# New engine orders for a fused attention and gated feed-forward kernel

## Chip, cores and metric

The kernel runs on one core of one Trainium2 chip. The metric is device time in microseconds (us), the median of several executions. The engines are named as in the profile: PE (TensorE, with PEld for its weight loads), DVE (VectorE), ACT (ScalarE), POOL (GpSimd), SP (SyncE, which here only issues DMAs).

## The reference

Two branches work on the same input x (2048 tokens of 512 numbers, bf16) and are mixed by a gate per token. Shortened:

```python
g = sigmoid((x * gate_w).sum(-1))              # one number per token
out = g * A(x) + (1 - g) * B(x)

def B(x):                                       # 512 -> 1792 -> 512
    return (gelu(x @ w_gate) * (x @ w_up)) @ w_down

def A(x):                                       # 32 heads of 16, 4 segments of 512 tokens
    q, k, v = x @ wq, x @ wk, x @ wv            # per head and segment
    for s in range(4):
        p = softmax(q_s @ k_s.T / 4 + causal mask)
        a_dot = p @ v_s
        a_mem = (phi(q_s) @ M) / (phi(q_s) @ z + 1e-6)     # memory of earlier segments
        o_s = sigmoid(beta) * a_mem + (1 - sigmoid(beta)) * a_dot
        M, z = M + phi(k_s).T @ v_s, z + phi(k_s).sum()
    return o @ wo                               # phi(t) = t + 1 if t > 0 else exp(t)
```

## The kernel before

The program works in four segments of 512 tokens and is one straight stream of instructions per engine, without loops on the chip. The build cuts the work into 630 named PE tasks and some 580 named tasks of the other engines. A written list per engine, `ORDER`, says in which order each engine works its tasks off. Each engine takes its list strictly in order; a task that must wait holds back all that stand behind it on its engine. The waits themselves are semaphores that `Emitter` places from the reads and writes of the tasks, so another order is another set of waits for the same work.

The names on PE, with segment first: `K0_2.1`, `Q1_3.0`, `V0_1.2` are pieces of the projections (piece .0 uses the first two blocks of 128 of the 512 input columns, piece .2 the last two; in segment 0 the K pieces are single matmuls of 256 columns). `G` and `U` are the gate and up projections (14 column tiles each), `D` the output of a token tile (its pieces take `wo` times attention, then `wd` times the feed-forward; in the last segment the other way round). `num` is phi(q) times the memory, `mz` the sum of phi(k) times v, 128 PE instructions in a row. `qk1_2A0` is a score fill: eight small matmuls (32 for a low fill, `L`) on four row groups of the array, into the four PSUM banks `psXALL`. `pv1_2_0` is a P*V task of 32 matmuls. Each matmul is two instructions on PE, the weight load and the matmul.

All tasks but the score fills share four more PSUM banks, `psW`. A bank is given to a task's group when its first piece comes up, and it is free again when a copy on ACT or DVE has read it: `Kev`, `Qev`, `Vev`, `Gev` are such copies, `Um` multiplies the up projection into the gelu, `pvt` transposes P*V, `fin` scales an output tile. Many copies may be on ACT or on DVE, and the two lists decide it.

Each fill is read by one exp (`exp1_2A0`, ACT) over all four banks of `psXALL`, so the next fill must wait for it; POOL then masks the result (`msk`). Between two fills PE usually has five pieces. Once per segment ACT changes to gelu and back, with a table load each way.

On SP stand the loads of x and of the weights (wk and wq are issued on ACT; `x2_1` loads one quarter of segment 2's x with a DMA transpose, `xt1` loads segment 1's x untransposed), copies within the chip (`pkT`, `oTd` transpose, `Vlo` copies V rows) and the stores (`out`). A load of w_up, w_down, wo or x2 has a "tick" among its reads: it waits for a named exp, so that loads don't all go out at once. `Vlow` and the x buffers are reused by later segments, and their loads wait for the last reader.

`Sched.schedule` walks the lists with estimated costs. With the lists given, its estimates decide only which of the four banks each group gets and in which order tasks of different engines are entered. Among its constants are `BLOCK`, `BLOCK_ASK` and `BLOCK_END` (when PE's code is fetched), `DMA_RATE`, and the byte counts that are passed with each load.

Of the kernel before, what the change touches and what calls it, by code (L numbers as in the profile page):

```python
# [7 lines left out]
PE, ACT, DVE, POOL, SP = "pe", "act", "dve", "pool", "sp"  # L8
# [26 lines left out]
BLOCK, BLOCK_ASK, BLOCK_END = 256, 165, 208  # L35
# [3 lines left out]
        "K0_2.0 K0_3.0 K0_0.1 K0_1.1 K0_2.1 K0_3.1 x0t0_1 x0t1_1 K0_0.2 K0_0.3 K0_2.2 K0_3.2 K0_2.3 K0_1.2 K0_1.3 "  # L39
        "K0_1.4 K0_1.5 K0_1.6 K0_1.7 K0_0.4 K0_0.5 K0_0.6 K0_0.7 K0_3.3 K0_2.4 K0_2.5 K0_2.6 K0_3.4 K0_3.5 Q0_2.0 "  # L40
        "Q0_1.0 Q0_1.2 Q0_2.2 Q0_3.0 K0_2.7 Q0_3.2 K0_3.6 Q0_0.0 Q0_0.2 K0_3.7 V0_1.0 V0_1.2 V0_0.0 V0_0.2 "
        "qk0_0A0 G0_5.0 G0_5.2 V0_3.0 V0_2.0 V0_2.2 qk0_0B0 V0_3.2 Q1_3.0 Q1_3.2 G1_10.0 G1_10.2 qk0_0L G0_1.0 "
        "G0_1.2 G0_9.0 G0_9.2 G0_7.0 qk0_0A1 G1_9.0 Q1_0.0 G0_4.0 G1_9.2 G0_4.2 qk0_0B1 G0_7.2 G1_7.0 G1_7.2 "
        "Q1_0.2 G1_1.0 G1_1.2 qk0_1A0 G1_11.0 G1_5.0 G1_5.2 G1_11.2 Q1_1.0 qk0_1B0 G0_6.0 G1_2.0 Q1_1.2 G0_10.0 "
        "G1_2.2 qk0_1A1 G0_6.2 K1_2.0 G0_10.2 pv0_0_1 pv0_0_0 qk0_1B1 K1_2.2 K1_1.0 G1_8.0 Q1_2.0 Q1_2.2 qk0_2A0 "
        "G1_8.2 K1_1.2 G0_8.0 G0_8.2 G0_3.0 qk0_2B0 V1_2.0 G0_3.2 V1_2.2 pv0_1_1 pv0_1_0 qk0_2L mz0 V1_0.0 "
        "G0_13.0 V1_0.2 qk0_2A1 G0_13.2 V1_3.0 G1_12.0 V1_3.2 G0_2.0 qk0_2B1 G1_12.2 G1_0.0 G0_2.2 G1_0.2 G0_0.0 "
        "G0_0.2 qk0_3A0 K1_0.0 G1_6.0 G1_6.2 K1_0.2 G0_12.0 qk0_3B0 K1_3.0 G0_12.2 K1_3.2 Q2_2.0 Q2_2.2 qk0_3A1 "
        "G1_3.0 G1_3.2 G0_11.0 G0_11.2 pv0_2_1 pv0_2_0 qk0_3B1 V1_1.0 Q2_0.0 Q2_0.2 Q2_3.0 Q2_3.2 G1_13.0 V1_1.2 "
        "G1_4.0 G1_4.2 G1_13.2 U0_1.0 U0_1.2 U0_2.0 U0_4.0 U0_2.2 U0_9.0 U0_0.0 U0_4.2 U0_0.2 qk1_0A0 U0_9.2 "  # L50
        "U0_3.0 U0_3.2 U0_7.0 U0_7.2 U0_10.0 U0_8.0 U0_8.2 U0_13.0 U0_13.2 U1_0.0 U1_0.2 U0_5.0 U0_10.2 U0_5.2 "
        "U1_13.0 num1_00.0 U1_1.0 U1_1.2 U1_10.0 U1_13.2 U1_10.2 U0_6.0 U1_7.0 U0_6.2 U1_5.0 U1_7.2 U1_2.0 "
        "qk1_0B0 U1_5.2 U1_2.2 U1_11.0 pv0_3_0 pv0_3_1 qk1_0L U0_11.0 Q2_1.0 Q2_1.2 U1_3.0 U0_11.2 qk1_0A1 U1_3.2 "
        "D0_0.0 D0_0.2 num1_01.0 D0_0.4 U1_11.2 qk1_0B1 U0_12.0 num1_02.0 U0_12.2 D0_0.6 D0_0.8 D0_2.0 qk1_1A0 "
        "D0_0.10 U1_8.0 U1_6.0 U1_8.2 U1_6.2 D0_0.12 qk1_1B0 D0_0.14 D0_2.2 D0_0.16 D0_2.4 D0_2.6 qk1_1A1 D0_2.8 "
        "num1_12.0 num1_10.0 num1_11.0 D0_2.10 D0_2.12 D0_2.14 qk1_1B1 D0_2.16 U1_12.0 U1_9.0 U1_9.2 U1_12.2 "
        "qk1_2A0 pv1_0_0 pv1_0_1 pv1_1_1 mz1 pv1_1_0 qk1_2B0 D0_1.0 D0_1.2 D0_1.4 D0_1.6 D0_1.8 V2_3.0 qk1_2L "
        "D0_1.10 D0_1.12 D0_1.14 D0_1.16 V2_3.2 qk1_2A1 V2_0.0 D0_3.0 U1_4.0 K2_0.0 U1_4.2 qk1_2B1 V2_0.2 D0_3.2 "
        "K2_3.0 D0_3.4 K2_0.2 qk1_3A0 K2_3.2 K2_1.0 D0_3.6 K2_2.0 K2_1.2 qk1_3B0 K2_2.2 D0_3.8 V2_1.0 D0_3.10 "
        "D0_3.12 qk1_3A1 D0_3.14 D0_3.16 V2_1.2 Q3_1.0 Q3_1.2 G2_0.0 qk1_3B1 pv1_2_0 pv1_2_1 G2_0.2 G2_1.0 G2_3.0 "  # L60
        "G2_2.0 G2_3.2 G2_1.2 G2_2.2 G2_6.0 G2_6.2 G2_7.0 G2_4.0 G2_4.2 G2_5.0 G2_5.2 qk2_0A0 pv1_3_0 pv1_3_1 "
        "G2_7.2 G2_8.0 G2_10.0 G2_8.2 G2_10.2 G2_9.0 G2_9.2 G2_11.0 G2_12.0 G2_11.2 G2_12.2 G2_13.0 G2_13.2 "
        "U2_9.0 U2_9.2 num2_01.0 U2_8.0 U2_8.2 D1_0.0 D1_0.2 num2_00.0 D1_0.4 U2_13.0 U2_13.2 qk2_0B0 num2_02.0 "
        "D1_0.6 D1_0.8 D1_0.10 D1_0.12 D1_0.14 U2_6.0 qk2_0L D1_0.16 U2_3.0 U2_0.0 U2_0.2 U2_6.2 qk2_0A1 U2_3.2 "
        "Q3_0.0 V2_2.0 D1_2.0 V2_2.2 qk2_0B1 Q3_0.2 num2_11.0 num2_10.0 D1_2.2 D1_2.4 D1_2.6 D1_2.8 qk2_1A0 "
        "Q3_3.0 Q3_3.2 D1_2.10 D1_2.12 U2_10.0 qk2_1B0 V3_0.0 U2_10.2 V3_0.2 Q3_2.0 Q3_2.2 qk2_1A1 U2_1.0 U2_7.0 "
        "num2_12.0 U2_7.2 D1_2.14 U2_1.2 qk2_1B1 V3_3.0 V3_3.2 U2_4.0 U2_4.2 D1_2.16 qk2_2A0 mz2 pv2_0_0 pv2_0_1 "
        "pv2_1_0 pv2_1_1 qk2_2B0 D1_3.0 D1_1.0 D1_1.2 D1_1.4 D1_1.6 qk2_2L D1_1.8 D1_3.2 D1_1.10 D1_3.4 V3_1.0 "
        "qk2_2A1 V3_1.2 D1_3.6 K3_2.0 D1_1.12 D1_3.8 qk2_2B1 D1_1.14 D1_3.10 K3_2.2 D1_1.16 K3_3.0 qk2_3A0 "
        "D1_3.12 U2_11.0 U2_11.2 K3_3.2 D1_3.14 qk2_3B0 K3_1.0 K3_1.2 V3_2.0 D1_3.16 K3_0.0 qk2_3A1 K3_0.2 G3_0.0 "  # L70
        "U2_5.0 U2_5.2 U2_12.0 V3_2.2 U2_12.2 qk2_3B1 pv2_2_1 pv2_2_0 G3_0.2 G3_1.0 G3_1.2 G3_2.0 G3_3.0 G3_3.2 "
        "G3_2.2 G3_4.0 G3_4.2 G3_8.0 G3_5.0 G3_5.2 G3_6.0 G3_6.2 G3_7.0 G3_9.0 G3_7.2 G3_9.2 G3_8.2 G3_10.0 "
        "G3_10.2 G3_12.0 G3_11.0 G3_11.2 G3_12.2 G3_13.0 G3_13.2 U3_5.0 qk3_0A0 U3_5.2 U3_9.0 U2_2.0 U3_7.0 "
        "U3_7.2 U2_2.2 U3_9.2 U3_10.0 qk3_0B0 pv2_3_1 pv2_3_0 U3_10.2 U3_4.0 qk3_0L U3_3.0 U3_3.2 U3_8.0 D2_0.0 "
        "U3_8.2 qk3_0A1 U3_4.2 D2_0.2 D2_0.4 D2_0.6 D2_0.8 qk3_0B1 num3_00.0 D2_0.10 num3_02.0 U3_2.0 U3_2.2 "
        "D2_0.12 num3_01.0 qk3_1A0 D2_0.14 D2_0.16 U3_6.0 D2_1.0 D2_1.2 qk3_1B0 D2_1.4 U3_6.2 D2_1.6 U3_0.0 "
        "U3_0.2 num3_10.0 qk3_1A1 U3_13.0 num3_11.0 U3_13.2 D2_1.8 D2_1.10 D2_1.12 num3_12.0 qk3_1B1 D2_3.0 "
        "D2_1.14 D2_3.2 D2_1.16 U3_1.0 qk3_2A0 pv3_0_0 pv3_0_1 D2_3.4 D2_3.6 U3_1.2 qk3_2B0 D2_3.8 D2_2.0 pv3_1_0 "
        "pv3_1_1 qk3_2L D2_3.10 D2_2.2 D2_3.12 D2_2.4 D2_3.14 qk3_2A1 D2_3.16 D3_0.0 D3_0.2 U3_12.0 D2_2.6 "
        "qk3_2B1 D2_2.8 U3_11.0 U3_11.2 D2_2.10 D2_2.12 qk3_3A0 D3_1.0 D3_0.4 D3_0.6 D2_2.14 D2_2.16 qk3_3B0 "  # L80
        "D3_1.2 U3_12.2 D3_0.8 D3_0.10 D3_1.4 qk3_3A1 pv3_2_0 pv3_2_1 D3_1.6 D3_2.0 qk3_3B1 pv3_3_0 D3_0.12 "
        "D3_2.2 D3_1.8 D3_2.4 D3_3w1.0 D3_1.10 D3_3w1.4 pv3_3_1 D3_3w1.8 D3_2.6 D3_0.14 D3_2.8 D3_1.12 D3_3w0.0 "
        "D3_3w1.12 D3_1.14 D3_3w0.4 D3_0.16 D3_1.16 D3_3w0.8 D3_2.10 D3_3a1.0 D3_2.12 D3_2.14 D3_2.16 D3_3w0.12 "
        "D3_3a0.0 "),
    "act": (
        "w_wk0 w_wk1 w_wq0 w_wq1 tload K0_0even K0_0ev pke0_0 Q0_2ev kl0_01 Q0_3ev kl0_21 kl0_20 Vev0_1 K0_3ev "
        "exp0_0A0 kl0_00 exp0_0B0 gexp Vev0_2 exp0_0L Gev0_1 exp0_0A1 gsum0_2 exp0_0B1 pke0_1 exp0_1A0 gexs0 "
        "exp0_1B0 Q1_1ev exp0_1A1 pqe1_0 exp0_1B1 K1_2ev exp0_2A0 Gev0_8 exp0_2B0 pqe1_1 exp0_2L Gev0_3 exp0_2A1 "
        "Vev1_3 exp0_2B1 Gev1_0 Gev0_2 exp0_3A0 K1_0ev exp0_3B0 Gev0_0 exp0_3A1 Q2_2ev gexs1 Gev0_11 exp0_3B1 "
        "gelu0_0 Gev1_4 gelu0_2 gelu0_6 gelu0_10 gelu1_0 gelu1_7 exp1_0A0 kl1_01 exp1_0B0 exp1_0L Q2_1ev exp1_0A1 "  # L90
        "pke1_0 exp1_0B1 exp1_1A0 pke1_1 exp1_1B0 fin0_0 exp1_1A1 exp1_1B1 fin0_2 exp1_2A0 pqe2_0 exp1_2B0 pqe2_1 "
        "exp1_2L fin0_1 exp1_2A1 exp1_2B1 gsum2_1 exp1_3A0 exp1_3B0 K2_3ev K2_2ev exp1_3A1 gexs2 exp1_3B1 gelu2_0 "
        "gelu2_1 gelu2_2 gelu2_3 gelu2_4 gelu2_5 gelu2_6 gelu2_7 kl2_00 gelu2_8 gelu2_9 gelu2_10 gelu2_11 "
        "gelu2_12 gelu2_13 exp2_0A0 exp2_0B0 pke2_0 exp2_0L fin1_0 exp2_0A1 pke2_1 exp2_0B1 Q3_0ev exp2_1A0 "
        "exp2_1B0 exp2_1A1 exp2_1B1 exp2_2A0 pqe3_0 exp2_2B0 exp2_2L exp2_2A1 Vev3_1 exp2_2B1 K3_2ev exp2_3A0 "
        "K3_3ev exp2_3B0 gsum3_2 exp2_3A1 pqe3_1 gexs3 exp2_3B1 gelu3_0 gelu3_1 gelu3_2 gelu3_3 gelu3_4 gelu3_5 "
        "gelu3_6 kl3_01 gelu3_7 gelu3_8 gelu3_9 gelu3_10 gelu3_11 gelu3_12 gelu3_13 exp3_0A0 exp3_0B0 exp3_0L "
        "exp3_0A1 exp3_0B1 exp3_1A0 fin2_0 exp3_1B0 exp3_1A1 exp3_1B1 fin2_1 exp3_2A0 exp3_2B0 exp3_2L exp3_2A1 "
        "exp3_2B1 exp3_3A0 exp3_3B0 fin2_2 exp3_3A1 exp3_3B1 fin3_0 fin3_30 "),
# [1076 lines left out]
```

## Time and profile before

| | |
|---|---|
| time, median of 3 | 270.37 us (269.36 to 270.85) |
| the profiled execution | 270.25 us |
| its span, first to last instruction | 268.5 us |
| granted TensorE clock | 1.0 |
| PE busy | 262.4 us (98%), 3021 matmuls |
| ACT busy | 210.5 us (78%) |
| DVE busy | 202.2 us (75%) |
| POOL busy | 105.1 us (39%) |
| DMA | 18.23 MB, mean 68 GB/s |
| read from HBM, written | 9.84 MB, 2.10 MB |

A line of the timeline gives the start and the length in us, the engine, the source line, the operation, what is written and read, the shape, the number of instructions merged, and in brackets the idle time ahead with what ended it. "issue" there means that the engine waited for nothing that the profile shows. Most matmuls come from one helper, so they share line 497; fills are line 860, exps 866, P*V 908 and 916, `mz` 828, copies 511 (ACT) and 514 (DVE). Ends of matmuls are modelled, so the distance from start to start is the better measure of PE.

### The profile page before, as it was taken

The page shows a single profiled execution, that of the slowest core. Times are in us where ns is not written, and L with a number is a line of the kernel's source. Part 1 is how long each engine was busy: PE and PEld are TensorE (multiplying, and loading weights), DVE is VectorE, ACT ScalarE, POOL GpSimd, SP SyncE. Part 2 cuts the span into 40 slices and gives each one's busy share as a digit, 9 for nine tenths or more (in the row PEclk, how much of TensorE's full clock was granted, in tenths as well). Part 3 has the DMA queues.
Part 4 walks back from the last instruction along what each step waited for, and adds up shares of the span by engine and source line. Part 5 has one row for each costly group of instructions (what it writes and reads, how often), then busy time and mean ns, then how long its engine had stood idle before and what let it go on. Part 6 is the DMA issues. An engine that isn't in the chain of part 4 may idle for free.

```text
span 268.5 us, 7155 instructions
## 1 busy us (share of the span) xinstructions
PE 262.4 (98%) x3021; PEld 119.2 (44%) x3021; DVE 202.2 (75%) x399; ACT 210.5 (78%) x180; POOL 105.1 (39%) x256
## 2 busy tenths in 40 slices
PE   8999999999999999899999999999999999999995
PEld 4543345334444435433444443543444444443452
DVE  1689989878988897868985877897691885685662
ACT  2689899989998987788868897779888768776801
POOL 8106582785200346161520628313771072326310
DMA  6950732892000055520000146230000002400002
GB/s 221 319 148 0 172 89 24 256 295 78 2 0 2 1 85 126 147 63 2 0 2 0 22 88 75 61 101 20 2 1 2 2 0 62 99 23 22 22 1 78
DMA packets 32752, 18.23 MB, mean 68 GB/s; under 512 B 20560, under 2 KB 32720, under 8 KB 32720
## 3 DMA queue, kind: packets, MB, share of 16 engines
q1 hardware_dynamic: 31632, 16.73, 25.6%
q10 hardware_dynamic: 1088, 1.05, 1.2%
q8 instruction: 23, 0.38, 0.6%
q14 instruction: 9, 0.07, 0.1%
HBM read 9.84 MB, written 2.10 MB: 44 GB/s over the span
## 4 chain that ended last, share of the span: by engine, by line
PE 90%; DMA 5%; SPq 2%; ACT 1%; issue 1%; ACTq 1%
PE psW L497 71%; PE psXALL L860 9%; PE psW L908 6%; DMA wq<-in_A_wq_dram 3%; PE psXALL L497 3%; DMA xT<-in_A_x_dram 2%; SPq L524 2%; PE psW L916 1%; ACT ptl L866 1%; ACTq L528 1%; PE psW L828 0%; SPq L528 0%; ACT ost L1036 0%; ACT hT L511 0%; ACTq L393 0%
## 5 line engine op out<-in xcount | busy, mean ns | idle before, releaser
L866 ACT ACTIVATE pt<-psXALL 128x2048 bf16<-128x2048 f32 x64 | 120.1, 1877 | 27.3 <-PE psXALL L860 24.5
L869 POOL TENSOR_SCALAR_AFFINE_SELECT pt<-pt 128x256 bf16<-128x256 bf16 x128 | 55.3, 443 | 111.9 <-ACT pt L866 107.0
L497 PE MATMUL psW<-xT,wu 128*128 128x512 bf16 x224 | 55.9, 380 | 0.0
L497 PE MATMUL psW<-wd,hT 128*128 128x512 bf16 x210 | 55.3, 380 | 0.0
L497 PE MATMUL psW<-xT,wg 128*128 128x512 bf16 x224 | 53.7, 380 | 0.0
L1007 DVE TENSOR_TENSOR hT<-psW,hT 128x512 bf16<-128x512 f32 x56 | 37.1, 684 | 19.1 <-PE psW L497 18.8
L869 POOL TENSOR_SCALAR_AFFINE_SELECT ptl<-ptl 128x512 bf16<-128x512 bf16 x32 | 23.9, 746 | 29.1 <-ACT ptl L866 27.4
L497 PEld LDWEIGHTS psW<-xT,wg 128*128 128x128 bf16 x224 | 20.6, 98 | 25.8 <-issue 1.9
L497 PEld LDWEIGHTS psW<-xT,wu 128*128 128x128 bf16 x224 | 20.7, 98 | 24.2 <-issue 1.7
L497 PEld LDWEIGHTS psW<-wd,hT 128*128 128x128 bf16 x210 | 18.4, 98 | 21.2 <-issue 2.7
L922 DVE STREAM_TRANSPOSE tb<-psW 128x512 f32<-128x512 f32 x32 | 21.7, 701 | 8.0 <-PE psW L916 7.7
L860 PE MATMUL psXALL<-qT,kpad 32*128 32x320 bf16 (+3 forms) x512 | 25.7, 273 | 1.3 <-issue 1.3
L860 PEld LDWEIGHTS psXALL<-qT,kpad 32*128 32x128 bf16 x512 | 7.7, 92 | 26.3 <-ACT pt L866 15.7
L908 PE MATMUL psW<-pt,vaug 128*17 128x192 bf16 (+3 forms) x512 | 18.8, 273 | 0.0
L991 ACT ACTIVATE hT<-psW 128x512 bf16<-128x512 f32 x28 | 15.3, 596 | 4.5 <-PE psW L497 4.5
L771 POOL COPY exsT<-exs 32x4 f32<-32x4 f32 x64 | 15.4, 240 | 8.2 <-ACT exs L762 4.6
L866 ACT ACTIVATE ptl<-psXALL 128x2048 bf16<-128x2048 f32 x8 | 15.0, 1877 | 4.5 <-PE psXALL L860 4.4
L497 PE MATMUL psW<-wv,xT 128*128 128x512 bf16 x64 | 18.1, 380 | 0.0
L497 PE MATMUL psW<-xT,wk 128*128 128x512 bf16 (+1 forms) x80 | 18.0, 337 | 0.0
L497 PE MATMUL psW<-wo,oT 128*128 128x512 bf16 x60 | 16.7, 379 | 0.1
L514 DVE CAST hT<-psW 128x512 bf16<-128x512 f32 x20 | 13.5, 686 | 4.3 <-PE psW L497 4.3
L908 PEld LDWEIGHTS psW<-pt,vaug 128*17 128x17 bf16 x512 | 10.4, 90 | 8.0 <-issue 3.0
(101 smaller groups left out, 310.7 us busy)
## 6 DMA issues: line engine op xcount, KB each, us to landing
out_dram<-ost SPq DMA_DIRECT2D x15, 128.0 KB, 2.0
wg<-in_B_w_gate_dram SPq DMA_DIRECT2D x2, 896.0 KB, 7.1
wu<-in_B_w_up_dram SPq DMA_DIRECT2D x2, 896.0 KB, 7.1
wd<-in_B_w_down_dram SPq DMA_DIRECT2D x2, 896.0 KB, 6.4
phkt<-in_A_x_dram SPq DMA_DIRECT2D x3, 512.0 KB, 5.1
vlow<-vaug SPq DMA_DIRECT2D x8, 136.0 KB, 2.7
wk<-in_A_wk_dram ACTq DMA_DIRECT2D x2, 256.0 KB, 4.6
hT<-in_A_x_dram SPq DMA_DIRECT2D x2, 256.0 KB, 4.2
```

The costliest lines, as they stand in the source:

```text
L497: return Instr(lambda e: e.matmul(view(), lhsT, rhs, start=first, stop=last), reads=reads, writes=[fkey if fkey is not None else g.key], e ...
L514: alts[DVE] = [Instr(lambda e: e.tensor_copy(dst(), src()), reads=reads, writes=writes, est=dve_t(n))]
L524: return e.dma_start_transpose(out_ap(), in_ap())
L528: return e.dma_start(out_ap(), in_ap())
L771: cross = task(f"exsT{s}", POOL, [Instr(lambda e, g=g, c=c: e.tensor_copy(exsT[sl][32 * g:32 * g + 32, c:16:4], exs[32 * c:32 * c + 32, s4 ...
L860: instrs.append(Instr(lambda e, g=g, lhs=lhs, rhs=rhs, c0=c0, ncol=ncol: e.matmul(X[g][:, c0:c0 + ncol], lhs(32 * g), rhs(32 * g), start=T ...
L866: exp_task(s, f"exp{s}_{t}{name}", [Instr(lambda e: e.activation(dst[:], XALL[:, :].rearrange("p (g c) -> p g c", g=4), ACTF.Exp, scale=AT ...
L869: task(f"msk{s}_{t}{name}", POOL, [Instr(lambda e, view=view, pat=pat, base=base: e.affine_select(out=view, in_=view, compare_op=ALU.is_ge ...
L908: instrs.append(Instr(lambda e, t=t, q=q, kb=kb, slot=slot, c0=c0: e.matmul(gp.f32()[32 * q:32 * q + 17, 128 * kb + 64:512], Vaug[sl][:, k ...
L922: task(f"pvt{s}_{t}_{j}", DVE, [Instr(lambda e: e.transpose(Tb[:, j, :], gp.f32()[:, :]), [gp.key], [("Tb", j)], dve_t(512))], grp=gp)
L991: lambda e, g=g, ft=ft, s=s: e.activation(hT[s % 2][:, ft, :], g.f32()[:, :], ACTF.Gelu_apprx_tanh),
L1007: task(f"Um{s}_{ft}", DVE, [Instr(lambda e, g=g, ft=ft: e.tensor_tensor(hT[sl][:, ft, :], g.f32()[:, :], hT[sl][:, ft, :], ALU.mult), [g.k ...
```

## The change

All five lists of `ORDER` are replaced. Every list of PE, POOL and SP holds the same tasks as before in another order; 30 tasks that ACT did are on DVE now and 30 that DVE did are on ACT. No task is added or removed, and no instruction is changed. The planner's constants and byte counts change too. The diff, cut to the constants, the places in the lists that the prediction speaks of, and the planner:

```diff
-BLOCK, BLOCK_ASK, BLOCK_END = 256, 165, 208
+BLOCK, BLOCK_ASK, BLOCK_END = 254.4, 172, 192
+DMA_SPARE = 1.6
+LANDING = {
+    "w_wk0": 4.8, "x0_0": 4.4, "w_wk1": 6.2, "x0_1": 5.8, "w_wq0": 8.2, "w_wv0": 7.4, "w_wq1": 10.1, "w_wv1": 8.9,
+    "w_wg0": 11.5, "x1_0": 12.1, "w_gwb": 12.4, "x1_1": 13.0, "w_beta": 13.3, "x1_2": 13.8, "x1_3": 14.3,
+}
 ORDER = {
     "pe": (
...
-        "K0_1.4 K0_1.5 K0_1.6 K0_1.7 K0_0.4 K0_0.5 K0_0.6 K0_0.7 K0_3.3 K0_2.4 K0_2.5 K0_2.6 K0_3.4 K0_3.5 Q0_2.0 "
-        "Q0_1.0 Q0_1.2 Q0_2.2 Q0_3.0 K0_2.7 Q0_3.2 K0_3.6 Q0_0.0 Q0_0.2 K0_3.7 V0_1.0 V0_1.2 V0_0.0 V0_0.2 "
-        "qk0_0A0 G0_5.0 G0_5.2 V0_3.0 V0_2.0 V0_2.2 qk0_0B0 V0_3.2 Q1_3.0 Q1_3.2 G1_10.0 G1_10.2 qk0_0L G0_1.0 "
...
-        "qk1_2A0 pv1_0_0 pv1_0_1 pv1_1_1 mz1 pv1_1_0 qk1_2B0 D0_1.0 D0_1.2 D0_1.4 D0_1.6 D0_1.8 V2_3.0 qk1_2L "
...
+        "K0_1.3 K0_1.4 K0_1.5 K0_1.6 K0_1.7 K0_3.4 K0_0.4 K0_0.5 K0_0.6 K0_0.7 K0_2.4 K0_3.5 Q0_1.0 K0_2.5 Q0_3.0 "
+        "Q0_0.0 K0_2.6 K0_2.7 Q0_2.0 Q0_1.2 Q0_2.2 Q0_0.2 V0_1.0 Q0_3.2 V0_1.2 K0_3.6 V0_0.0 qk0_0A0 V0_3.0 "
+        "K0_3.7 V0_3.2 V0_2.0 V0_0.2 V0_2.2 G1_1.0 qk0_0B0 G1_5.0 G0_4.0 G0_4.2 G0_5.0 G1_5.2 qk0_0L G0_8.0 "
...
+        "D0_2.16 pv1_0_0 pv1_0_1 qk1_2A0 V2_3.0 K2_0.0 V2_3.2 K2_0.2 U1_4.0 qk1_2B0 U1_4.2 mz1 pv1_1_1 pv1_1_0 "
...
     "sp": (
-        "x0_0 x0_1 w_wv0 w_wv1 w_wg0 x1_0 w_gwb x1_1 w_beta x1_2 x1_3 w_wg1 pkT0_0 pkT0_1 Vlo0_0 Vlo0_1 w_wu0 "
-        "pkT0_3 pkT0_2 x2_3 xt1 w_wd0 w_wu1 x2_0 x2_2 x2_1 w_wd1 w_wo x3_1 oTd1_0 Vlo1_1 pkT1_0 Vlo1_0 oTd1_1 "
...
+        "x0_0 x0_1 w_wv0 w_wv1 w_wg0 x1_0 w_gwb x1_1 w_beta x1_2 x1_3 w_wg1 pkT0_1 Vlo0_0 pkT0_0 Vlo0_1 pkT0_2 "
+        "pkT0_3 w_wu0 x2_2 x2_3 x2_1 xt1 x2_0 w_wu1 w_wo w_wd1 Vlo1_0 Vlo1_1 w_wd0 oTd1_0 oTd1_1 pkT1_0 out0 "
...
-            if t.nbytes:
+            if t.nbytes and t.name not in LANDING:
                 t.finish = max(t.finish, dma_free - DMA_BACKLOG)
...
-            if t.nbytes:
+            if t.name in LANDING:
+                avail = max(t.finish + 3.0, LANDING[t.name])
+                dma_free = max(dma_free, avail)
+            elif t.nbytes:
                 dma_free = max(t.finish + DMA_LAT, dma_free) + t.nbytes / DMA_RATE
-                avail = dma_free
+                avail = dma_free + DMA_SPARE
...
-                [], xkeys, 524288)
+                [], xkeys, 700000)
...
-        wdma(("wu", i), SP, wu[:, :, sl], wur[:, :, sl], 917504, reads=[("tick", 0, *e)])
+        wdma(("wu", i), SP, wu[:, :, sl], wur[:, :, sl], 1050000, reads=[("tick", 0, *e)])
...
-        wdma(("wd", i), SP, wd[:, 7 * i:7 * i + 7, :], wdr[:, 7 * i:7 * i + 7, :], 917504, reads=[("tick", 0, *e)])
-    wdma("wo", SP, wo[:], r4(A_wo), 524288, reads=[("tick", 0, 3, "A1")])
+        wdma(("wd", i), SP, wd[:, 7 * i:7 * i + 7, :], wdr[:, 7 * i:7 * i + 7, :], 1050000, reads=[("tick", 0, *e)])
+    wdma("wo", SP, wo[:], r4(A_wo), 600000, reads=[("tick", 0, 3, "A1")])
```

Other places of the new order that the prediction names: `qk0_2B0` is followed by `G0_10.2 mz0 pv0_1_0 pv0_1_1 qk0_2L`; `qk0_2B1` by `Q2_0.0`; `U1_10.2` by `pv0_3_1 pv0_3_0 qk1_0B0`; `qk1_0A1` and `qk1_0B1` by the first pieces of D0, with `D0_0.4` the first that needs `wd`; `qk2_1B1` by `pv2_0_0 mz2 pv2_0_1 pv2_1_0 qk2_2A0`, with `pv2_1_1` between the two next fills; `qk3_1B1` by `U3_1.0 num3_12.0 D2_1.16 U3_1.2 U3_0.0 qk3_2A0`.

## The prediction

> **What bounds the kernel now.** I read the page first, then the waits, the chain of waits, the timeline of TensorE and of its weight loads, and last the DMA issues. The page:
>
> ```profile
> span 268.5 us, 7155 instructions
> PE 262.4 (98%) x3021; PEld 119.2 (44%) x3021; DVE 202.2 (75%) x399; ACT 210.5 (78%) x180; POOL 105.1 (39%) x256
> PE 90%; DMA 5%; SPq 2%; ACT 1%; issue 1%; ACTq 1%
> ```
>
> TensorE (PE) carries 90% of the chain, so only two things move the end: PE's own work, and the places where PE stands still. A busy share of 98% doesn't find those places, because the end of a matmul is modelled; start-to-start distances do. The cadence from the timeline:
>
> ```profile
> 230.09 0.59 PE L497 MATMUL psW<-wd,hT 128*128 128x512 bf16 x2
> 230.52 0.59 PE L497 MATMUL psW<-wo,oT 128*128 128x512 bf16 x2
> ...
> 231.39 0.59 PE L497 MATMUL psW<-xT,wu 128*128 128x512 bf16 x2
> 231.91 0.40 PE L860 MATMUL psXALL<-qT,kpad 32*128 32x448 bf16 x8
> 232.24 0.62 PE L908 MATMUL psW<-pt,vaug 128*17 128x448 bf16 x16
> ...
> 232.80 0.61 PE L908 MATMUL psW<-pt,vaug 128*17 128x448 bf16 x16
> ```
>
> A piece of two 512-column matmuls takes 0.43 (230.09 to 230.52). A score fill of eight takes 0.33, a P*V task 0.56. A change between full-array, score and P*V work costs 0.10 more (0.52 instead of 0.43 ahead of the fill). I laid these steps along the whole old order; what the trace has beyond them is idle PE, and nearly all of it sits in a few places:
>
> ```profile
> 10.49 0.98 PEld L497 LDWEIGHTS psXALL<-xT,wq 128*128 128x128 bf16 x6 [0.93 <-DMA wq<-in_A_wq_dram]
> 27.91 0.55 PEld L497 LDWEIGHTS psW<-xT,wg 128*128 128x128 bf16 x4 [0.53 <-DVE hT L514]
> 58.37 0.33 PEld L497 LDWEIGHTS psW<-xT,wq 128*128 128x128 bf16 x3 [0.90 <-DMA xT<-in_A_x_dram]
> 110.42 0.39 PE L860 MATMUL psXALL<-qT,kpad 32*128 32x320 bf16 x5 [1.28 <-issue]
> 175.04 0.31 PEld L497 LDWEIGHTS psW<-wo,oT 128*128 128x128 bf16 x2 [0.43 <-issue]
> ```
>
> The bracket holds the gap of the engine; the loss, from matmul starts, is another number. They are: 0.60 for the second half of wq (`Q0_1.2`; 0.82 between starts instead of 0.22), 0.65 for x2 (`Q2_2.0`), 1.58 and 0.31 of "issue", 0.20 for a PSUM bank that VectorE freed late (`G1_1.0`), 0.09 for a fill right behind a low fill (`qk0_2A1`), and 0.32 between the P*V tasks of segments 1 and 2. Together **3.75 us**. That is all a new order can win on PE; it adds and removes no instruction.
>
> **The change, part by part.** *Start.* The DMAs of the first 13 us keep their order, so the landings stay. Ahead of `Q0_1.2` the new order has one more K piece (0.11) and two more first halves of Q (0.87), which need the first half of wq alone. PE used to arrive at 9.90 and now arrives at 10.87; the half landed by 10.49. Gain 0.60, margin 0.4. ScalarE takes two of the five x0 copies; it waited 4.25 ahead of its first copy, so they cost nothing, and two of them (about 1.0 by its 0.59 copies) still end before `K0_0.2` at 6.74. The first fill comes at 15.25 - 0.60 - 0.54 (a V and a K piece go behind it) = 14.1.
>
> *x2.* On SP three of the four transposes stood behind an 896 KB load of wd and one of wu (x2_0 issued 48.99, landed 57.34). Now three of them go out once `exp0_1B1` is done, at about 39 by the cadence, and the fourth behind xt1 alone, which must wait for `mz0` (44.7); so it is issued at about 45.1. First user is now `Q2_0.0`, at 51.2. With the median landing of 4.2 us that is 49.3, margin 1.9; with the 8.35 us of the crowded old case it is 53.5 and PE would wait 2.3. Only xt1 (512 KB) is beside it, so I take the median: gain 0.65.
>
> *wd.* Its first half moves on SP behind Vlo1_0 and Vlo1_1, and these wait for the last readers of the V buffer, `pv0_3_1` and `pv0_3_0` (end 82.1). So SP stands there with wd, the next transposes and the outputs queued behind. Two issues of 0.62, and wd goes at 83.4; first user is `D0_0.4`, at 91.7. That allows 8.3. The 896 KB loads landed 5.2 to 9.0 after issue (9.0 in the crowd of the start), so the cost is 0, at worst 0.7.
>
> *"Issue".* PE stopped at its 2,476th and 4,004th instruction, 1,528 apart, six times 254.7; the 23 packets of queue q8 (0.38 MB, 16.4 KB each) landed at 108.89 and 173.75, and PE went on 1.5 and 1.3 later. This is the fetch of PE's own code, one block at a time, and a burst eats a block fast: `pv1_0_0 pv1_0_1 pv1_1_1 mz1 pv1_1_0` is 384 instructions in 3.3 us. By the new constants the request goes out 274 instructions ahead of the boundary; counted back, that is 106.66 and 171.36, so a fetch takes 3.76 and 3.68 us. In the new order I took the time PE needs for the 274 ahead of each of the boundaries: the shortest are 4.8 (`qk1_2A0` to `pv1_1_0`), 5.2 (`qk0_2A0` to `pv0_1_1`), 6.5 and 6.6 (around `mz2`); all others are above 8. Old: without the stops about 2.0 and 3.4 at these two, and 5.4 at a third, which passed. Gain 1.89, with 0.32 for the gaps inside those bursts 2.21.
>
> The Trainium skill, "Runtime: NRT & Kernel Launch", section "Instruction fetch mechanics", speaks against this part: it has the code refilled in blocks of 256 instructions by the engine's own queue, and calls a crossing mostly hidden. The block agrees with 254.7; "hidden" doesn't, with 1.58 of idle beside it. By that rule alone the two stops would be something else that stays, and the forecast would be 1.9 higher.
>
> *ScalarE between fills.* A fill must find its scores read: 0.52 from fill to exp, 1.88 for the exp, 0.05 to the next fill, 2.45 in all. Five pieces and a fill give 2.6. In the new order I put, fill by fill, the PE time beside the exp plus what ScalarE has to do before the next; the worst cases are short by 0.1 to 0.3, as in the old order, and the next interval makes it up. One interval is too short on PE itself: `qk3_1B1` to `qk3_2A0`, 2.28. Cost 0.17. The gelu stretch of segments 0 and 1 keeps its reserve (`qk0_3B1` to `qk1_0B0` 20.75 after 20.9, of which 0.97 was spare).
>
> *VectorE and the banks.* Thirty tasks go from ScalarE to VectorE and thirty back, so the engines' sums stay. But PE runs the stretch from the first P*V to segment 1's in 68.2 instead of 70.4, and VectorE was busy 61.1 of the 70.2 from 36.0 to 106.2. I followed the four banks by hand through 14 to 32, 61 to 83, 103 to 116 and 187 to 197: handovers come 0.1 to 0.6 ahead of the next user. So some will be late. Below, 0: a wait gives nothing back. Above, 2.0, were each of some 20 tight handovers 0.1 late. The nearest rows are the old 0.20 and 0.09; I take **0.5**, because there are more tight ones.
>
> *Rest.* Changes of array mode rise from 159 to 160: 0.10. At the end two output copies go to ScalarE, which stood idle 6.4 and 3.3 us ahead of its last two; the closing work (`D3_3w0.12 D3_3a0.0`, the last copy and store) is as before: 0. The new planning constants add no instruction; they choose banks.
>
> Sum: 268.5 - 3.75 + 0.10 + 0.17 + 0.5 = 265.5 of span. The profiled execution took 270.25, 1.7 more than its span, and lies 0.1 under the median: 267.2, so **267.4** against the median.
>
> **The rivals.** *The idle moves into the banks* (no change): VectorE, fuller by 2 points, frees banks late in many places, and 1.6 to 4.3 come back in pieces: 269.0 to 271.7. For it: 87% busy before, and waits on VectorE's copies exist. Against: it had lost 0.29 in all, and its in-order head waits were on PE.
>
> *Slower: the code fetch is longer than two stops tell.* Both were seen with few transfers about. The new boundary at `pv0_1_1` falls among wu, x2 and xt1, the one at `pv1_1_0` among transposes. At 7.0 us a fetch, the four short windows lose 2.2 + 1.8 + 0.5 + 0.4 = 4.9: 272.3. It decides from about 6.8 us. Against it: the old 5.4 window passed with x2_3 in flight.
>
> *A load is late after all* (x2_0 or wd): 2.3 or 0.7 more, 268.1 to 270.4; and *the order is followed but the stops don't follow the counting*, so that 1.9 stays: 269.3.
>
> **How the numbers follow.** The measurement can tell about 0.5%, 1.35 us, from no change: faster is under 269.0, slower over 271.7. Forecast, with a late load or a few more bank waits inside it: 0.75. The no-change cases together 0.14. Slower 0.11, 0.06 of it the fetch, the rest several waits that add up. The likeliest case spans 266.2 (no new wait, and 0.4 of scatter) to 268.9; the range goes to 270.0, which leaves out about 0.2.
>
> **What the profile would show.** Right: no 0.93 ahead of wq nor 0.90 ahead of xT, no "issue" gap over 0.5 on PE or its loads past 100 us, first fill near 14.1, first fill of segment 3 near 202.6 (206.8 before), one short gap near 227. Wrong: "issue" gaps near 45 or 109; many weight loads waiting 0.3 to 0.6 for a VectorE copy between 36 and 104; a wait for wd near 92 or x2 near 51.

## The result and the profile after

The new order takes 267.32 us (median of 6, 267.05 to 267.54) where the kernel before took 270.61 beside it (median of 6, 269.36 to 273.45): a ratio of 0.9888, 95% interval 0.9854 to 0.9922. On a second chip it took 266.96 (5 executions, 266.47 to 267.37) against 270.45: 0.9871, 0.985 to 0.9893. The ratios leave out executions over 1.5% above the fastest of the same kernel (here 273.45, without which the median before is 270.37). The forecast was 267.4. The profiled execution took 267.31, and the lines of its page that answer to those of before are:

```profile
span 265.6 us, 7154 instructions
PE 261.7 (99%) x3021; PEld 119.5 (45%) x3021; DVE 201.2 (76%) x399; ACT 209.8 (79%) x182; POOL 109.0 (41%) x256
PE 96%; DMA 2%; ACT 1%; issue 0%; ACTq 0%
```

PE has 96% of the chain instead of 90%, and the 5% of DMA (x2 and wq), 2% of SP and 1% of "issue" have shrunk to the first loads of x. Busy time is nearly what it was. In the waits of the matmuls over the whole span, one row is left, the warm-up at the start:

```profile
engine line waited for: us in total, times, longest us
PE psW L590 <- PEq L1169: 0.8, 1, 0.8
```

Laying the steps of PE along the order, as in the prediction, leaves 0.67 us beyond them (4.2 before), and one place over 0.1. It is in the timeline of PE, at the fill that the forecast named:

```profile
227.04 1.03 PE L505 MATMUL psW<-xT,wu 128*128 128x512 bf16 x4
228.18 0.40 PE L868 MATMUL psXALL<-qT,kpad 32*128 32x448 bf16 x8
228.51 0.61 PE L916 MATMUL psW<-pt,vaug 128*17 128x448 bf16 x16
```

Four matmuls take 0.87 by the cadence and the change of mode 0.10; from 227.04 to 228.18 are 1.14, so the fill `qk3_2A0` stood 0.18 late. The weight loads show the two transfers that used to stop PE:

```profile
10.80 1.07 PEld L505 LDWEIGHTS psXALL<-xT,wq 128*128 128x128 bf16 x6
...
51.73 0.55 PEld L505 LDWEIGHTS psW<-xT,wq 128*128 128x128 bf16 x4 [0.21 <-DMA xT<-in_A_x_dram]
```

The second half of wq meets no wait (the bracket of 0.93 is gone). x2 still has a bracket, 0.21 of the load queue, none of it lost on PE: `x2_0` landed at 51.65 and its user started at 51.74. That is no margin, where the forecast had 1.9.

### The profile page after: what moved, and what is told of

It is laid out like the page before. It is cut to its first block, busy times and chain, and to the rows that moved or that the text cites. A ratio compares the mean times of both kernels' runs of the same rounds, so it can differ in the third digit from the quotient of the medians.

```text
span 265.6 us, 7154 instructions
## 1 busy us (share of the span) xinstructions
PE 261.7 (99%) x3021; PEld 119.5 (45%) x3021; DVE 201.2 (76%) x399; ACT 209.8 (79%) x182; POOL 109.0 (41%) x256
## 4 chain that ended last, share of the span: by engine, by line
PE 96%; DMA 2%; ACT 1%; issue 0%; ACTq 0%
PE psW L505 76%; PE psXALL L868 9%; PE psW L916 6%; PE psXALL L505 3%; DMA hT<-in_A_x_dram 2%; PE psW L924 1%; PE psW L836 1%; ACT pt L874 1%; PE psXALL L599 0%; ACT ost L1044 0%; PE psW L590 0%; ACTq L401 0%
## 5 line engine op out<-in xcount | busy, mean ns | idle before, releaser
L877 POOL TENSOR_SCALAR_AFFINE_SELECT pt<-pt 128x256 bf16<-128x256 bf16 x128 | 57.5, 460 | 72.1 <-ACT pt L874 67.2
L779 POOL COPY exsT<-exs 32x4 f32<-32x4 f32 x64 | 16.7, 261 | 3.7
L522 DVE CAST hT<-psW 128x512 bf16<-128x512 f32 x19 | 12.6, 682 | 2.2 <-PE psW L505 2.1
```

The lines of the kernel that those rows point to most:

```text
L522: alts[DVE] = [Instr(lambda e: e.tensor_copy(dst(), src()), reads=reads, writes=writes, est=dve_t(n))]
L779: cross = task(f"exsT{s}", POOL, [Instr(lambda e, g=g, c=c: e.tensor_copy(exsT[sl][32 * g:32 * g + 32, c:16:4], exs[32 * c:32 * c + 32, s4 ...
L877: task(f"msk{s}_{t}{name}", POOL, [Instr(lambda e, view=view, pat=pat, base=base: e.affine_select(out=view, in_=view, compare_op=ALU.is_ge ...
```

## The experiments

All are whole kernels. "Old" is the kernel before, "new" the changed one. Each ratio is to the kernel before beside it on the same chip; the rows come from several chips, on which the kernel before alone had medians from 269.92 to 270.61. The last column is PE from the first K matmul (`K0_0.0`) to the end of its last matmul in the profiled execution: it leaves out how late PE started. In the three executions that started at 6.02 it holds 0.2 to 0.3 of half clock at the start.

| kernel | median us (range) | ratio to before, 95% | `K0_0.0` at | PE from there |
|---|---|---|---|---|
| old | 270.61 (269.36 to 273.45) | 1 | 5.41 | 260.25 |
| new | 267.32 (267.05 to 267.54) | 0.9888 (0.9854 to 0.9922) | 5.88 | 256.82 |
| new, second chip | 266.96 (266.47 to 267.37) | 0.9871 (0.985 to 0.9893) | 5.46 | 256.82 |
| old, code shifted by 192 | 268.34 (267.43 to 269.27) | 0.9928 (0.9902 to 0.9954) | 6.02 | 257.81 |
| old, code shifted by 256 | 273.99 (270.76 to 274.18) | 1.0131 (1.0092 to 1.017) | 5.67 | 263.41 |
| new, code shifted by 160 | 271.61 (271.1 to 272.31) | 1.0061 (1.0036 to 1.0086) | 5.81 | 261.15 |
| old, x2 early | 269.47 (268.88 to 270.41) | 0.9965 (0.9941 to 0.9989) | 5.42 | 258.85 |
| old, Q halves moved | 270.75 (269.53 to 273.91) | 1.0022 (1.0005 to 1.004) | 6.02 | 260.13 |
| old, x2, Q and 192 | 267.88 (267.41 to 268.86) | 0.9934 (0.9908 to 0.996) | 5.67 | 257.10 |
| old, x2, Q and 256 | 269.51 (268.58 to 271.9) | 0.9972 (0.9947 to 0.9997) | 5.46 | 259.60 |
| new, old order of loads | 274.41 (274.26 to 274.95) | 1.017 (1.0143 to 1.0198) | 6.02 | 264.31 |
| the same, wait filled | 272.41 (271.81 to 273.17) | 1.0077 (1.0055 to 1.0098) | 5.89 | 262.03 |
| new, four copies twice | 268.52 (267.46 to 268.81) | 0.9937 (0.9912 to 0.9961) | 5.21 | 257.81 |
| new, one piece earlier | 267.47 (267.11 to 268.62) | 0.9898 (0.9874 to 0.9923) | 5.07 | 257.97 |

**Are the "issue" stops the fetch of code, and does its phase decide?** The matmuls of some tiles are cut from 512 columns into two of 256. That adds PE instructions at nearly the same matmul time (0.437 for a pair of pieces instead of 0.433), and moves what follows against the blocks of 254.7 instructions. First the old order with 24 tiles cut, 192 instructions ahead of segment 1's P*V:

```diff
+SPLIT = set("U0_0 U0_1 U0_2 U0_3 U0_4 U0_5 U0_6 U0_7 U0_8 U0_9 U0_10 U0_11 U0_12 U0_13 "
+            "U1_0 U1_13 U1_1 U1_10 U1_7 U1_5 U1_2 U1_11 U1_3 U1_8".split())
+    def cols(name):
+        return [slice(0, 256), slice(256, 512)] if name in SPLIT else [slice(0, 512)]
-            pieces(f"U{s}_{ft}", g, [mm(g, lambda g=g: g.f32()[:, :], wu[:, kb, ft * 128:(ft + 1) * 128],
-                                        xT[x3][:, kb, :], [*xk(s, kb), ("w", ("wu", ft // 7))], kb == 0,
-                                        kb == 3, 512) for kb in range(4)], 2)
+            pieces(f"U{s}_{ft}", g, [mm(g, lambda g=g, c=c: g.f32()[:, c], wu[:, kb, ft * 128:(ft + 1) * 128],
+                                        xT[x3][:, kb, c], [*xk(s, kb), ("w", ("wu", ft // 7))], kb == 0,
+                                        kb == 3, c.stop - c.start)
+                                     for c in cols(f"U{s}_{ft}") for kb in range(4)], 2)
```

> The old order, unchanged; only 96 of its U matmuls of 512 columns (in 24 U tiles worked between 62 and 97 us) are cut into two of 256 columns each, which puts 192 more PE instructions into the stream at the same matmul time (0.109 x 2 against 0.2165, so about +0.2 us in all). Every later boundary of the code blocks then falls 192 instructions earlier in the program. Theory (the issue stops are the fetch of PE's code, 3.7 us from a request 274 instructions ahead): the bursts at segments 1 and 2 no longer lie in a short window; both stops go, span 268.5 - 1.9 - 0.2 + 0.2 = 266.7, time about 268.4. Rival (the stops belong to the burst itself, P*V and mz back to back, whatever the phase of the blocks): both stops stay, span 268.7, time about 270.5.

Measured 268.34, a span of 266.7: more matmuls, and faster. Both stops behind the P*V tasks were gone. At the first place the fill runs through (8 matmuls in one line; before, 1.58 lay between its third and its fourth):

```profile
107.01 0.61 PE L916 MATMUL psW<-pt,vaug 128*17 128x448 bf16 x16 [0.26 <-ACT ost L1062]
...
108.88 0.40 PE L868 MATMUL psXALL<-qT,kpad 32*128 32x320 bf16 x8
```

The wait in the first line is another matter: `pv1_1_1` needs a bank that ScalarE's copy of an output tile frees late. It stands in six of the seven profiles with the old order (0.22 by starts in the kernel before, 0.43 here), and it doesn't go with the stops. The cut matmuls change no bank: in every shifted kernel each group has the bank it had. Then the new order, which has no stop, with 20 tiles cut (V and G, 160 instructions):

```diff
+SPLIT = set("V0_0 V0_1 V0_2 V0_3 G1_1 G1_5 G0_4 G0_5 G0_8 G0_3 "
+            "G1_2 G1_10 G1_11 G0_1 G1_0 G1_9 G1_7 G0_7 G0_9 G0_6".split())
```

> The new order, unchanged; only 80 of its V and G matmuls of 512 columns (20 tiles worked before 37 us) are cut into two of 256 columns, 160 more PE instructions, about +0.2 us of matmul time. Theory (code fetch): now three boundaries fall just behind the bursts at pv0_1/mz0, mz1 and mz2, and PE stops with 'issue' three times, 1.5 to 1.9 each, sum 5.6 (from 4.5 to 6): span about 271.3, time about 273. Rival (the new order is free of stops because its bursts are broken up): no stop over 0.3, span 265.8, time 267.5.

Measured 271.61, slower than the kernel before, but 1.4 under the expectation. The timeline of PE of this kernel has the stops in the three bursts, and the bracket names "issue":

```profile
48.35 0.21 PE L876 MATMUL psXALL<-qT,klow 32*128 32x64 bf16 x5 [1.65 <-issue]
...
114.11 0.20 PE L876 MATMUL psXALL<-qT,klow 32*128 32x64 bf16 x2 [1.18 <-issue]
...
172.10 0.25 PE L924 MATMUL psW<-pt,vaug 128*17 128x192 bf16 x4 [0.66 <-issue]
```

By starts they cost 1.86, 1.41 and 0.92. They stand in the middle of fills and P*V tasks of 32 small matmuls, and the profile shows no engine or load that PE waited for. The direction had to be tested too: is it the phase, or do the cut matmuls help by themselves? The old order with a whole block more:

```diff
+SPLIT = set("U0_0 U0_1 U0_2 U0_3 U0_4 U0_5 U0_6 U0_7 U0_8 U0_9 U0_10 U0_11 U0_12 U0_13 "
+            "U1_0 U1_13 U1_1 U1_10 U1_7 U1_5 U1_2 U1_11 U1_3 U1_8 "
+            "V1_0 V1_1 V1_2 V1_3 G1_13 G1_4 G0_11 G1_3".split())
```

> The kernel before with 256 extra instructions of TensorE ahead of segment 1's P*V (32 tiles of 512 columns as two of 256), where the faster version had 192. Theory (the phase of the code blocks decides): 256 is one whole block of 254.7, so the boundaries fall where they fell before, one block later in number; the stop of about 1.6 us behind segment 1's P*V tasks comes back, and some 0.3 to 0.6 in segment 2: ratio 0.998 to 1.002, 269.6 to 270.6 us against 270.1. Rival (the extra instructions or the halved matmuls themselves help, the phase doesn't matter): as with 192, ratio 0.993 or below, 268.2 us.

Both stops came back (1.21 and 0.77), but the time missed the expectation by 4 us: x2 was late as well, and more happened there than a wait (the clock, below). So the pair was run once more with x2 early, 192 against 256 instructions. The 192 version is also the test whether the parts add up (besides the `SPLIT` sets above; the lists are cut to the places that change):

```diff
     "sp": (
-        "x2_3 xt1 w_wd0 w_wu1 x2_0 x2_2 x2_1"
+        "x2_3 x2_0 x2_2 x2_1 xt1 w_wd0 w_wu1"
     "pe": (
-        "Q0_2.0 Q0_1.0 Q0_1.2 Q0_2.2 Q0_3.0 K0_2.7 Q0_3.2 K0_3.6 Q0_0.0 Q0_0.2"
+        "Q0_2.0 Q0_1.0 K0_2.7 Q0_3.0 Q0_0.0 Q0_1.2 Q0_2.2 Q0_3.2 K0_3.6 Q0_0.2"
```

> The kernel before with three edits and no other change of order: the 192 extra instructions of TensorE in segment 0's and 1's U products (each 512-column matmul of 24 tiles cut into two of 256), the three x2 transposes ahead of the loads of wd and wu on SyncE, and the two halves of Q moved ahead of the second half of wq. Theory: these stops are all that the new order removes, and they are worth the same together as apart. The first edit alone gave a ratio of 0.9928 and the second 0.9965; together 0.989, so about 267.2 us and a span near 265.6, as in the new order. Rival 1: with the fetch stops gone, TensorE meets the x2 transposes no later than they land (as the profile of the first edit alone had it), so nothing is added: ratio 0.993, 268.2 us. Rival 2: the new order wins something else as well (wider margins of the banks), and this kernel stays 0.5 to 1 us behind it.

> The kernel of the three edits (x2 transposes early, halves of Q moved, U products cut) with 256 extra instructions of TensorE ahead of segment 1's P*V instead of 192. With 256 alone, the stops behind the P*V tasks were back (1.21 and 0.77 us, where 192 had none), but that kernel also met x2 late and lost clock, so it settled nothing by its time; here x2 is early. Theory (the phase of the code blocks decides): those two stops, about 2.0 us more than the 267.88 of the three edits with 192: 269.7 to 270.0 us. Rival (the cut matmuls or the extra instructions help by themselves): 267.9 or below.

267.88 with 192 (0.9934), 269.51 with 256 (0.9972, on another chip). The only difference is 64 more instructions, and PE's timeline of the second has the two old stops in the old places:

```profile
109.64 0.39 PE L872 MATMUL psXALL<-qT,kpad 32*128 32x320 bf16 x5 [1.20 <-issue]
...
174.44 0.81 PE L503 MATMUL psW<-wo,oT 128*128 128x512 bf16 x3 [0.34 <-issue]
```

By starts 1.50 and 0.50, against 1.58 and 0.31 in the kernel before. The phase decides: in two orders and five positions of the blocks, the stops go, come and move as the count says. At two instructions a matmul, the stops of the new order shifted by 160 stand at PE's 1,204th, 2,730th and 4,002nd instruction, those here at the 2,732nd and 4,260th. With the 2,476th and 4,004th of the kernel before, all seven lie within 4 instructions of one grid, 1,204 plus 254.4 a block. And each time a packet of the code queue q8 had landed 1.3 to 1.5 us before PE went on (at 47.02, 112.74 and 170.65, and here at 108.30 and 173.06).

As a sum of parts the 192 version missed its theory: 0.9934 (0.9908 to 0.996) and not 0.989. It isn't clearly faster than the cut matmuls alone (0.9928), as rival 1 had it, and stays 0.6 to 0.9 us behind the new order, as rival 2 had it.

**x2 and the Q halves by themselves.** Each of the two edits of lists above alone, in the old order:

> The old order with one edit on SP: x2_0, x2_2 and x2_1 go ahead of xt1, w_wd0 and w_wu1 (they were behind them). Theory (each stall on PE is worth its own length): x2 lands by about 47 to 50 instead of 58.3, the 0.65 at Q2_2.0 goes, nothing else moves; span 267.9, time 269.6. Rival (the stall only covers another wait that is late next, such as DVE's copies or ScalarE's exps): the 0.65 goes at 58 and comes back within 10 us; span 268.5, time 270.3.

> The old order with one edit on PE: the pieces behind the second half of wq are put later (Q0_2.0 Q0_1.0 K0_2.7 Q0_3.0 Q0_0.0 Q0_1.2 Q0_2.2 Q0_3.2 K0_3.6 Q0_0.2). Theory: PE arrives at Q0_1.2 about 1.0 later in work and finds wq landed; the 0.60 goes, first fill at 14.65 instead of 15.25; span 267.9, time 269.7, unless x0 lands later than in the old profile. Rival (the first fill waits for the copies of Q0 and K0 anyway): the 0.6 turns into a wait ahead of the first fill at 15.25; span 268.5, time 270.3.

x2 early gave 269.47, a ratio of 0.9965; the gap at 58 was gone and the stop at 109 stayed (1.43). The Q halves gave nothing, 270.75 and a ratio of 1.0022. In that profile the waits on wq were gone, but the first fill still came at 15.54, because PE had started late: `K0_0.0` at 6.02. The same start is in the profile with 192 instructions, which has the old order of Q, and there PE didn't wait for wq either. With the old order of Q the wait was 0.60, 0.09, 0 and 0 in four profiled executions (`K0_0.0` at 5.41, 5.42, 5.67, 6.02). When PE starts late, the half is there in time in any order.

**Does the new PE order need the new order of loads?** The new lists with the x2, wd and wu loads of the old one (cut to the places that change):

```diff
     "sp": (
-        "x2_2 x2_3 x2_1 xt1 x2_0 w_wu1 w_wo w_wd1 Vlo1_0 Vlo1_1 w_wd0"
+        "x2_3 xt1 w_wd0 w_wu1 x2_0 x2_2 x2_1 w_wd1 w_wo Vlo1_0 Vlo1_1"
```

> The new order on all engines, with the loads of the old order between x2 and wd on SyncE: one x2 transpose, xt1, the first half of wd, the second half of wu, then the other three x2 transposes. Theory: x2_0 then goes out near 47.5 us instead of 45.7 and, beside 1.8 MB of weights, lands near 56 (57.3 in the old order); its first user stands at 51.8, so TensorE waits 4 to 5 us ahead of segment 2's first Q piece: span near 270, about 271.7 us, slower than both. It would show that the new PE order needs the new order of the loads. Rival (a load's place on the queue hardly matters, transposes pass the weights): under 0.7 us of wait, 267.3 to 268.0 us.

It does: 274.41, 2.7 above the expectation. The wait for x2 was 5.05 by starts, near the 4 to 5 expected, but 2.1 more were lost behind it. PE's timeline there, and PE by windows (the columns are the window, its length, PE busy and instructions, granted clock, share of the DMA engines, GB/s):

```profile
57.14 0.61 PE L509 MATMUL psW<-xT,wq 128*128 128x512 bf16 x1 [4.98 <-DMA xT<-in_A_x_dram]
58.04 1.46 PE L509 MATMUL psW<-xT,wq 128*128 128x512 bf16 x3 [0.28 <-DMA xT<-in_A_x_dram]
59.29 1.06 PE L509 MATMUL psW<-wv,xT 128*128 128x512 bf16 x2
60.15 1.06 PE L509 MATMUL psW<-xT,wg 128*128 128x512 bf16 x2
```

```profile
52.00:54.00 2.00, 0.16 (x8) 1.00 2.21 357
54.00:56.00 2.00, 0.00 (x0) 0.57 1.05 36
56.00:57.00 1.00, 0.00 (x0) 0.50 0.92 186
...
60.00:61.00 1.00, 1.00 (x4) 0.50 0.00 0
61.00:62.00 1.00, 0.97 (x11) 0.95 0.00 0
```

A piece takes 0.86 (59.29 to 60.15) where it takes 0.43 elsewhere, and the granted clock is 0.50 until 61. That is some 1.65 of the 2.1; the rest, 0.47, is a second wait for x2, ahead of the second matmul (58.04). To see whether idleness is the cause, PE got something to do in that wait: the product V1_0 just ahead of it is computed seven times, with the same values.

```diff
+            more = [Instr(m.fn, m.reads, m.writes, m.est) for _ in range(6) for m in instrs] \
+                if f"{name}.{i}" == "V1_0.2" else []
-            r = task(f"{name}.{i}", PE, instrs[i:i + size], grp=g, after=after, bias=bias)
+            r = task(f"{name}.{i}", PE, instrs[i:i + size] + more, grp=g, after=after, bias=bias)
```

> The new order with the old order of the x2 and wd loads, which waited 5.05 us for x2 and then ran its matmuls at half clock for about 4 us (2.1 us lost), and in that wait something for TensorE to do: the product of V1_0, just ahead of the wait, is computed seven times over instead of once (24 more matmuls of 512 columns, 5.2 us; the same values each time). Theory (idle TensorE loses its clock): no idle, no half clock; x2 lands when it did, so the end is 2 us earlier than 274.4: 272.3 us, and the granted clock stays 1.00 between 54 and 62 us. Rival (the half clock comes from something else, as the transfers of the weights): the clock falls as before, 274.4 us or more.

Measured 272.41: 24 matmuls more, and 2.0 us faster (on another chip). PE had no wait for x2 left, so the 0.47 is in the gain too; most of it is the clock. The windows of this kernel:

```profile
54.00:56.00 2.00, 2.00 (x11) 1.00 0.56 93
56.00:57.00 1.00, 1.00 (x13) 1.00 0.55 112
...
60.00:61.00 1.00, 1.00 (x6) 1.00 0.03 8
```

**How much reserve have the banks?** Four copies of VectorE done twice in the new order:

```diff
+            if name in "Gev0_7 Gev0_13 Gev1_8 Gev1_4".split():
+                alts[DVE].append(Instr(lambda e: e.tensor_copy(dst(), src()), reads=reads, writes=writes,
+                                       est=-GAP[DVE]))
```

> The new order with four copies of VectorE done twice (the G copies Gev0_7, Gev0_13, Gev1_8, Gev1_4, 0.69 us each, between 40 and 62 us). It measures the reserve of the PSUM banks, priced at 0.5 us in the forecast. Theory: a copy delays PE only by what exceeds the distance between the end of the copy and the first matmul of the bank's next user. In the trace of the new order the first copy has 1.3 us and more behind it on every bank it delays: nothing. The other three fall into one stretch with distances of 0.40, 0.46, 0.52 and 0.37: waits of about 0.35, 0.6, 0.4 and 0.15, in all 1.5 us: 268.8 us. Rival 1 (VectorE has 24% idle and catches up): under 0.3, 267.3 to 267.6. Rival 2 (the whole chain of VectorE is tight and each copy comes through): 2.1 to 2.8 us, about 269.8.

268.52, and 0.99 more on PE than in the new order. By starts the four waits were 0.38 (`G0_11`), 0.16 (`G0_12`), 0.27 (`U0_1`) and 0.14 (`G1_13`), 0.95 in all; the first copy cost nothing. Both rivals fall. The distances price a late bank rightly in place, but gave 1.5 for 0.95: after the first wait, the rest of the delay was absorbed sooner than I had followed it.

**A version that beats both?** The 0.18 ahead of `qk3_2A0`, by one piece more in front of the fill (the start of the edit; the pieces behind it move by one place until the end of segment 3):

```diff
-        U3_0.0 qk3_2A0 pv3_0_0 pv3_0_1 U3_0.2 D2_3.0 qk3_2B0 D2_3.2 D2_3.4 pv3_1_1
+        U3_0.0 U3_0.2 qk3_2A0 pv3_0_0 pv3_0_1 D2_3.0 D2_3.2 qk3_2B0 D2_3.4 D2_3.6 pv3_1_1
```

> The new order with the one short gap between fills made longer: a piece of U more ahead of the fill qk3_2A0, which was 0.18 us late for ScalarE, and the pieces behind it each one place earlier until the end of segment 3. A try at a version that beats both. Theory: the 0.18 us of idle at 228 goes and nothing comes back: span 0.18 less, 267.1 us, a ratio to the new order of 0.9993, hardly measurable. Rival: the later pieces meet their banks or scores earlier than these are free, and 0.1 to 0.5 comes back: 267.3 to 267.7.

> The new order, unchanged, on the chip of the three others, so that they have it beside them. Theory: 267.3 us and a spread of a few tenths; the first fill between 14.0 and 15.0, by how early TensorE gets its full clock. The three edits alone (267.88 on another chip) would then lie 0.5 us behind the new order. Rival: on this chip it shows the same spread as the kernel before (over 1.5 us).

267.47 beside 266.96 for the unchanged new order: not better. The 0.18 went, and 0.42 at `D2_3.0` and 0.45 at `D3_3w1.0` came, as the rival said, though it had named 0.1 to 0.5. Another 0.45 of this execution was a wait for x2 (`Q2_0.0`), which the edit doesn't touch:

```profile
230.06 1.04 PE L509 MATMUL psW<-wo,oT 128*128 128x512 bf16 x4 [0.35 <-DVE tb L934]
251.57 0.72 PE L509 MATMUL psXALL<-wd,hT 128*128 128x128 bf16 x6 [0.29 <-ACT pt L878]
```

At `D2_3.0` the piece moved forward was the one that had kept the bank's next user behind a VectorE transpose. No kernel here is faster than the new order.

## Why the prediction was right, and where it was not

The time came out as forecast and the main steps held, but the sum has two errors that cancel; that it hit to 0.1 us is luck. From `K0_0.0` to the last matmul PE took 3.43 us less (260.25 to 256.82). The forecast's terms without the bank term give 3.75 - 0.10 - 0.17 = 3.48. The bank term of 0.5 was not there, and PE started 0.47 later than in the profile of before, which the forecast didn't have.

*"Issue" (2.21 of gain): the 1.89 right, and shown.* No gap of "issue" above 0.5 on PE or its loads past 100 us, and the shifted kernels tie the stops to the blocks. Of the 0.32 that the prediction adds for gaps inside the bursts, 0.22 wasn't the fetch but the bank ahead of `pv1_1_1`, which ScalarE freed late; in the new order, where other tasks stand there, it is gone as well. The size of one stop was less sure than 3.76 and 3.68 suggested: with a fetch of 3.72, the cadence gives stops of 1.87, 1.87 and 1.85 for the new order shifted by 160; they were 1.86, 1.41 and 0.92, so a fetch took 2.8 to 3.7 us, at most what the two old stops told. The slower rival's 7 us is excluded. The rule weighed against this part (the Trainium skill, "Runtime: NRT & Kernel Launch", "Instruction fetch mechanics": a crossing of a block boundary is mostly hidden) differs from the runs: the new order lost 4.2 us at crossings when it was shifted by 160, and the measurement decides. The new planner constants have no part in it: built with the old ones, the new lists give every group the same bank.

*Start (0.60 of gain): the mechanism right, the size not.* The wait on wq belonged to the profiled execution. Of the other three executions with the old start two had none, and the edit alone gave nothing. What I took for a fixed stop of PE was the difference of two scattered times: PE's start (5.41 to 6.02) and the landing of the half (9.94 to 10.45). I had one execution and read a scatter as a constant. The first fill came at 14.57 instead of 14.1, and in the other kernels with the new start at 13.79 to 14.92, always 8.7 to 8.9 behind `K0_0.0`.

*x2 (0.65 of gain): the gain right, the margin not.* `x2_0` went out at 45.74, as forecast (45.1), but took 5.9 us and not the median 4.2. That median was over all transposes of x; the four of x2 alone had 6.2 in the old profile. And I had only xt1 beside it, where wu's second half went out at 46.96, right behind it. Where wu followed after 1.2 us, as here, x2_0 took 5.4 to 6.4 in three profiles; where it followed after 2.2 and 2.3, it took 4.6 and 4.4. The landings in kernels with the new loads were 49.95, 50.24, 50.49, 51.36 and 51.65; one of them (51.36, with an earlier PE) cost 0.45. For the old order, x2 was worth 0.6 by the medians and 0.95 by the ratio: its landing scattered (the last quarter at 57.14 to 59.66) around a user at 57.4 to 57.9, and the longest wait took another 1.5 of clock with it. With x2 early the old order ranged over 1.5 us, where the kernel before ranged over 3.5 beside it (269.02 to 272.51, and one execution of 25 at 273.57).

*Banks (0.5 of loss): wrong.* No such wait is in the trace. I had argued from handovers that come 0.1 to 0.6 ahead of the next user, and that these would be tighter with PE faster. Counted in both traces (220 handovers of the `psW` banks, from the end of the copy to the next user's first matmul), those under 0.2 us went from 10 to 4, those under 0.4 from 37 to 24, those under 0.7 from 98 to 71. I followed new distances and never counted the old ones: against them the new order is wider, not tighter. In these traces a wait stands only where the distance is under 0.1 (0.05 and 0.06, ahead of `pv1_1_1` and `G1_1.0` in the old order), and the copies done twice show what lies behind that.

*ScalarE (0.17), wd (0), changes of mode (0.10), the end (0).* The one late fill came where it was named, with 0.18. wd's first half went out at 84.75 and landed at 89.84; its user came at 92.25. The ends differ by 0.1.

*What stays open.* By the medians, the three edits explain between half and two thirds of the gain (2.0 us, or 1.8 by the ratio, of 3.0 to 3.5); their median stays 0.6 to 0.9 us behind the new order's. The profiled executions differ by only 0.28 on PE (0.20 of it the bank ahead of `G1_1.0`), but that of the three edits was the fastest of its six. These medians come from different chips, and the other executions weren't traced. How far the wider margins of the banks make up the rest isn't settled.

## What to carry to other kernels

Before costing a stop, look for it in more than one execution: a wait that is the difference of two scattered times (a landing and a late start) can be worth more or less on the median than one profile shows (0.60 here, and nothing by itself), and a margin forecast from a median landing must carry the landing's spread. For a handover, count the distances in the old trace as well as the new; only the difference says whether a new order is tighter. In a kernel bound by PE, bursts of small matmuls run through the code faster than it is fetched, so anything that adds or removes PE instructions upstream can cost or win microseconds (here 2 to 4 of 270) without being slow or fast itself.

## What the runs showed of the hardware

*An idle PE loses half its clock, for 3.4 us or twice that.* In the old order shifted by 256, PE stood 1.97 us for x2; then these windows of PE:

```profile
58.00:59.00 1.00, 0.00 (x0) 1.00 0.17 38
59.00:60.00 1.00, 0.29 (x2) 0.94 1.11 324
60.00:61.00 1.00, 1.00 (x7) 0.50 1.09 344
61.00:62.00 1.00, 1.00 (x12) 0.50 0.70 221
62.00:63.00 1.00, 1.00 (x7) 0.50 0.00 0
63.00:64.00 1.00, 1.00 (x9) 0.85 0.00 0
```

So a wait for x2 of 2.1 us (1.97, and 0.17 ahead of the first matmul) cost 3.85 by starts. The trace's clock record has the half clock from 59.89 to 63.30, which is 3.41 us, and it began 0.2 after PE had gone on. In the new order with the old loads it lasted from 54.26 to 61.09, twice 3.41, and began 2.1 into the wait. The stops of 1.65 us and less in the new order shifted by 160 left the clock at 1.00. The Trainium skill ("TensorE: Matmul & The Clock Gate", "Part 1: The HAM clock gate (the "warmup" mystery)") puts the loss at an idle window of some 3.4 us, free-running. The length agrees with the 3.41; but a whole idle window wasn't needed: 1.97 us of idleness was enough, and 1.65 wasn't, in these few traces. That the window runs freely agrees with the next point.

*The full clock comes at another time in each execution.* The first K matmuls of 256 columns follow each other by 0.11 from the start (old order, `K0_0.0` at 5.41), or by 0.21 until 6.45 (the Q halves moved, 6.02), though the profile's clock column says 1.00 there. In 11 of the 14 traces the clock record begins with the full clock, at 3.76 to 6.62, and `K0_0.0` follows it: 5.07 and 5.21 where it begins at 3.8, 5.42 to 5.89 where it begins at 4.7 to 5.8, 6.02 where it begins at 6.5 to 6.6. The end moves with `K0_0.0` unless a later wait takes it up.
